# Last tile's scratch in five parts, three of them reloaded in rounds 8, 11 and 14; last inverse in 12 chunks of 512 columns, eight last output writes

## The chip, the cores and the metric

One core of a Trainium2 chip. The metric is device time of one execution in microseconds. The core's engines run side by side, each with its own queue of instructions in program order: TensorE (PE in the profile; its weight loads are PEld), VectorE (DVE), ScalarE (ACT), GpSimd (POOL) and SyncE (SP). SP issues nearly all transfers between memory and the core; ACT issues a few.

## The reference

A 7x7 circular convolution of a 224 x 224 image of 96 channels, written with FFTs:

```python
def reference(x, w):
    ...
    Xf = rfft2(x)                                # over the two image axes
    Wf = rfft2(w padded to H x W)
    Yf = jnp.einsum('bhwi,hwio->bhwo', Xf, Wf)
    y = irfft2(Yf).astype(jnp.bfloat16)
    return y
```

Inputs are `x` (1, 224, 224, 96) and `w` (7, 7, 96, 96) in bfloat16, the output has the shape of `x`.

## The kernel before

The kernel transforms along the image's height only, in 8 row blocks of 28 rows, and does the width as a short convolution with Karatsuba-like tricks. The width is cut into seven tiles (t = 0 to 6) of 32 pixels. Each tile goes through three stages:

- **a** (forward): PE multiplies pixels by the constant `Fm`; DVE and ACT cast the result from PSUM into `xf`, the spectrum. There are two `xf` buffers, used in turn.
- **b**: 17 rounds, one for each frequency pair s = 0 to 16 (`b_round`). A round is 33 small matmuls of 96 columns on PE (22 in rounds 0 and 16), a scaled copy `tt_` on ACT, the sums `u` and `v` on DVE, and a last sum into `yf` on POOL or DVE (`ydve`: on DVE in the rounds that also make the next group's differences `J`, and in the last three rounds of the last tile). Three rounds share one `yf` tile, which is written to scratch in DRAM by a transfer (`put`).
- **c** (inverse): the scratch is read back with frequency on the partitions (`tt`), PE multiplies by the constant `G`, DVE and ACT cast the result into `yo` (or free space in a `J` buffer), and SP writes the output.

Stages overlap: while tile t is in its rounds, stage a of tile t+1 and stage c of tile t-1 are run as fill jobs between the matmuls of the rounds. `add(a, b, jobs)` spreads a list of jobs over the half rounds a to b (`pace`), two half rounds to a round. `CQ` says how many leftover and how many new c jobs each tile takes; `k1` is the half round in which the last of them is due. `pump` loads `tt` tiles when buffers are free.

The last tile (t = 6, `TL`) has nobody to hide its inverse, so its stage c is special. Its scratch lies in parts of their own. Its inverse takes all 8 row blocks at once: the sum over frequencies is split into a first half (rounds 0 to 8: constant `GA`, data `tl_a`, 72 partitions, one buffer for each four row blocks g) and a second half (rounds 9 to 16: constant `GB`, data `tl_b`, 128 partitions). `tl_a` and `tl_b` lie in the `xf` buffer of tile 5, which is free by then. `GA` and `GB` are filled from `G` by small transfers, one in each round of tiles 3 and 4 (`g_parts`).

In the last tile `put` goes on ACT's queue, one round late (the list `puts`), but for the last one, which SP issues. Before, the scratch has three parts: rounds 0 to 8 (reloaded in round 11 by four transfers), rounds 9 to 14 (two transfers on ACT's queue, after the rounds) and rounds 15 and 16 (one on SP). Then come, in PE's order: eight first halves (`first`, one to each PSUM bank), `WARM` matmuls on zeros that only keep PE busy, and the loop over 16 chunks of 384 columns: `second` completes a chunk, `tail_evac` casts it on DVE or ACT in turn, the remaining first halves come as banks are freed, and every four chunks SP writes 112 partitions x 1536 columns of the output.

A transfer signals its landing on one of eight completion semaphores, which are handed out in turn to all transfers, whether SP or ACT issues them; a transfer is issued only when the previous one on its semaphore has landed.

Every instruction is recorded by one helper (line 87; 89 in the changed file), so the profile's groups are told apart by tile names.

## Time and profile before

| | |
|---|---|
| timed, median of 3 runs | 275.37 us (274.2 to 276.08) |
| span of the profiled execution | 273.5 us |
| mean granted TensorE clock | 0.998 |
| bytes moved by transfers | 46.78 MB |
| idle POOL before its sums, most of it on nothing the profile shows | 88.0 us |

The chain that ended last is 72% PE, 11% DMA, 7% DVE and 5% ACT. The stretches of the end read as follows (busy us of each engine, granted clock, bytes per time):

| stretch, us | PE | DVE | ACT | clock | GB/s |
|---|---|---|---|---|---|
| 250 to 254 | 4.00 | 3.87 | 2.41 | 1.00 | 248 |
| 254 to 256 | 0.83 | 1.07 | 0.05 | 1.00 | 301 |
| 256 to 258 | 2.00 | 0.00 | 0.00 | 1.00 | 206 |
| 258 to 260 | 2.00 | 0.00 | 0.00 | 1.00 | 90 |
| 260 to 262 | 2.00 | 0.00 | 0.00 | 1.00 | 244 |
| 262 to 264 | 0.73 | 0.00 | 0.00 | 1.00 | 69 |
| 264 to 266 | 2.00 | 1.70 | 1.34 | 1.00 | 0 |
| 266 to 268 | 2.00 | 1.69 | 1.53 | 1.00 | 227 |
| 268 to 270 | 0.20 | 0.77 | 0.77 | 1.00 | 270 |

How to read it: in a profile line the first number is the start in us from the span's start, the second the length; `out<-in` are tiles with buffer numbers left out; `xN` counts instructions; what stands in brackets is the engine's idle time before and what ended it. SPq and ACTq are the issuing queues, and their lines give the time of issuing, not of the transfer. Busy PE from 256.66 to 262.67 is the warming matmuls.

### The profile page before, as it was taken

Reading aid. Unit: us, or ns where it says so; the run is one execution under the profiler, and the core shown is the slowest. Engines: PE = TensorE matmul, PEld = TensorE weight load, DVE = VectorE, ACT = ScalarE, POOL = GpSimd, SP = SyncE. Lnnn points to the kernel's source line nnn. Section 1 sums busy time; section 2 is a strip of 40 time slices with the busy share of each in tenths; the row PEclk is TensorE's granted clock in tenths of the full one; section 3 lists DMA queues with packets and bytes.
Section 4 is the critical chain, followed back from the end, with each engine's and each line's share of the span. In section 5 each row is a group of like instructions: output and inputs, shape, how many; then the busy total and the mean of one; then the engine's idle time right before and its main releaser. Section 6 shows DMA issues by size and latency. Waiting matters only on the chain.

```text
span 273.5 us, 12147 instructions
## 1 busy us (share of the span) xinstructions
PE 259.0 (95%) x5149; PEld 237.7 (87%) x5149; DVE 213.0 (78%) x455; ACT 197.2 (72%) x485; POOL 94.8 (35%) x156
## 2 busy tenths in 40 slices
PE   8989998999999999999999999999999999899882
PEld 3659898999999989999999989999999999789661
DVE  5629799898979889779787887787977998788232
ACT  5529997668785657988988889888988865666022
POOL 7780032336446523431422222224144314224000
PEclk9999999999999999999999999999999999999999
DMA  6956110641112398996968487889678644797765
GB/s 177 222 119 169 52 47 2 168 135 48 46 47 88 105 288 149 274 263 166 310 172 248 116 228 217 200 205 313 253 194 181 204 162 132 154 297 195 196 120 180
DMA packets 46038, 46.78 MB, mean 171 GB/s; under 512 B 35150, under 2 KB 36954, under 8 KB 45886
## 3 DMA queue, kind: packets, MB, share of 16 engines
q1 hardware_dynamic: 43696, 43.94, 58.9%
q10 hardware_dynamic: 2288, 2.06, 2.7%
q8 instruction: 40, 0.66, 1.1%
q14 instruction: 14, 0.11, 0.1%
HBM read 24.65 MB, written 21.33 MB: 168 GB/s over the span
## 4 chain that ended last, share of the span: by engine, by line
PE 72%; DMA 11%; DVE 7%; ACT 5%; issue 2%; SPq 1%; POOL 1%; DVEq 0%; ACTq 0%
PE pb L87 72%; DMA wq<-in_w_dram 5%; ACT WF L87 3%; DVE WF L87 2%; DVE J L87 2%; DMA xf<-scrb 2%; DMA tt<-scr 2%; DMA scrb<-yf 1%; SPq L87 1%; DVE u L87 1%; DMA scr<-yf 1%; DVE v L87 1%; ACT xf L87 1%; DVE yf L87 1%; POOL yf L87 1%
## 5 line engine op out<-in xcount | busy, mean ns | idle before, releaser
L87 PE MATMUL pb<-WF,J 96*128 96x96 bf16 x2821 | 163.1, 206 | 1.1 <-DVE J L87 0.6
L87 PEld LDWEIGHTS <-J 96*128 96x128 bf16 x2821 | 138.2, 98 | 9.8 <-DVE u L87 1.5
L87 POOL TENSOR_TENSOR yf<-v,u 128x384 bf16<-128x384 f32 x79 | 77.8, 999 | 151.3 <-issue 88.0
L87 ACT CAST xf<-pb 96x408 bf16<-96x408 f32 (+3 forms) x143 | 67.3, 488 | 8.1 <-PE pb L87 6.3
L87 PE MATMUL pb<-WF,xf 96*128 96x96 bf16 x952 | 60.3, 206 | 1.1 <-ACT xf L87 0.5
L87 DVE TENSOR_TENSOR J<-xf 96x1824 bf16<-96x1824 bf16 (+1 forms) x84 | 57.6, 725 | 0.1
L87 PEld LDWEIGHTS <-xf 96*128 96x128 bf16 x952 | 47.3, 98 | 1.8 <-issue 0.9
L87 PE MATMUL pb<-Fm,xn 118*128 118x136 bf16 (+3 forms) x640 | 45.5, 199 | 0.9 <-DVE u L87 0.8
L87 ACT CAST WF<-pb 96x480 bf16<-96x480 f32 (+1 forms) x59 | 29.1, 573 | 6.8 <-PE pb L87 6.8
L87 PE MATMUL pb<-tt,Gm 102*84 102x384 bf16 (+1 forms) x132 | 32.4, 326 | 1.3 <-DMA tt<-scr 1.3
L87 ACT CAST J<-pb 84x384 bf16<-84x384 f32 (+1 forms) x65 | 28.0, 484 | 6.0 <-PE pb L87 3.0
L87 ACT CAST yo<-pb 84x384 bf16<-84x384 f32 (+1 forms) x66 | 28.2, 484 | 5.1 <-PE pb L87 5.1
L87 PEld LDWEIGHTS <-xn 118*128 118x128 bf16 x640 | 30.5, 97 | 1.2 <-issue 1.1
L87 DVE TENSOR_TENSOR J<-J 96x912 bf16<-96x912 bf16 (+2 forms) x42 | 22.8, 542 | 0.0
L87 PE MATMUL pb<-wq 98*128 98x120 bf16 (+1 forms) x288 | 21.3, 226 | 1.0 <-DMA wq<-in_w_dram 1.0
L87 PEld LDWEIGHTS <-wq 98*128 98x128 bf16 x288 | 19.4, 150 | 1.4 <-issue 1.4
L87 PE MATMUL pb<-wu 128*128 128x512 bf16 (+1 forms) x80 | 18.3, 392 | 1.0 <-DVE ct L87 1.0
L87 PEld LDWEIGHTS <-wu 128*128 128x128 bf16 (+1 forms) x80 | 9.4, 120 | 8.8 <-issue 3.3
L87 DVE TENSOR_TENSOR yf<-v,u 128x384 bf16<-128x384 f32 x26 | 14.7, 566 | 0.9
L87 DVE CAST WF<-pb 96x480 bf16<-96x480 f32 (+1 forms) x13 | 7.5, 610 | 6.8 <-PE pb L87 6.7
L87 PEld LDWEIGHTS <-Gm 102*84 102x84 bf16 (+1 forms) x132 | 11.0, 117 | 2.0 <-DMA tt<-scr 1.4
L87 ACT CAST tt<-pb 112x384 bf16<-112x384 f32 x8 | 3.6, 479 | 11.1 <-PE pb L87 11.0
(385 smaller groups left out, 239.7 us busy)
## 6 DMA issues: line engine op xcount, KB each, us to landing
scr<-yf SPq DMA_DIRECT2D x30, 288.0 KB
xn<-in_x_dram SPq DMA_DIRECT2D x12, 672.0 KB
tt<-scr SPq DMA_DIRECT2D x24, 336.0 KB
out_dram<-yo SPq DMA_DIRECT2D x12, 252.0 KB
out_dram<-J SPq DMA_DIRECT2D x12, 252.0 KB
tt<-scr SPq DMA_DIRECT2D x6, 288.0 KB
wq<-in_w_dram SPq DMA_DIRECT2D x1, 1719.0 KB
WF<-in_x_dram SPq DMA_DIRECT2D x2, 672.0 KB
```

Source lines behind the costliest of these rows:

```text
L87: r = fn(*a, **k)
```

## The change

The last tile's scratch is cut into five parts, rounds 0 to 5, 6 to 8, 9 to 11, 12 to 14 and 15 to 16. The first three are reloaded inside the rounds (8, 11 and 14) on SP, the fourth after the rounds on ACT's queue, the fifth on SP. The rows of `GA` and `GB` are laid out for the parts. The fill jobs of the last tile are due by half round 24 instead of 28. The last inverse works in chunks of 512 columns instead of 384, 12 instead of 16; there are 22 warming matmuls instead of 36; and each group of three chunks is written out by two transfers, one of 1024 columns and one of 512.

```diff
-SB = 15
+LPART = ((0, 6), (6, 9), (9, 12), (12, 15), (15, 17))
+LROW = (0, 48, 0, 48, 96)
+LOADS = (8, 11, 14)
...
-WARM = 36
+WARM = 22
...
             if t == TL:
-                i = (s >= SA) + (s >= SB)
-                dst, yo0 = scr_tiles[(t, i)], (0, SA, SB)[i]
+                i = next(i for i, (p0, p1) in enumerate(LPART) if p0 <= s < p1)
+                dst, yo0 = scr_tiles[(t, i)], LPART[i][0]
...
-    def load_b(i, eng, nh):
-        sb = scr_tiles[(TL, 1 + i)].rearrange("w j s (r e) -> (j s r) w e", r=2)
-        for h in range(nh):
-            w0, w1 = h * TW // nh, (h + 1) * TW // nh
-            eng.dma_start(out=tl_b[i * KB[0]:i * KB[0] + KB[i], w0:w1], in_=sb[:, w0:w1])
+    def load_l(i, eng):
+        s0, s1 = LPART[i]
+        sv = scr_tiles[(TL, i)].rearrange("w j s (r e) -> (j s r) w e", r=2)
+        halves = [(tl_a[g], g, 2) for g in range(2)] if s0 < SA else [(tl_b, 0, 1)]
+        n = NJ * 2 * (s1 - s0) // len(halves)
+        for buf, g, _ in halves:
+            eng.dma_start(out=buf[LROW[i]:LROW[i] + n].rearrange("p (w e) -> p w e", w=TW), in_=sv[g * n:(g + 1) * n])
 
     def g_parts():
-        for j in range(4):
-            dma(GA[j * 2 * SA:(j + 1) * 2 * SA, j * B:(j + 1) * B], G[0:2 * SA, 0:B])
-            yield
-        for j in range(NJ):
-            for i, (s, s1) in enumerate(((SA, SB), (SB, NS))):
-                n = 2 * (s1 - s)
-                dma(GB[i * KB[0] + j * n:i * KB[0] + (j + 1) * n, j // 4, j % 4 * B:(j % 4 + 1) * B], G[2 * s:2 * s1, 0:B])
+        for i, (s0, s1) in enumerate(LPART):
+            n = 2 * (s1 - s0)
+            for j in range(4 if s0 < SA else NJ):
+                r0 = LROW[i] + j * n
+                o = GA[r0:r0 + n, j * B:(j + 1) * B] if s0 < SA else GB[r0:r0 + n, j // 4, j % 4 * B:(j % 4 + 1) * B]
+                dma(o, G[2 * s0:2 * s1, 0:B])
                 yield
...
-        k1 = 2 * NS if t < TL else 2 * NS - 6
+        k1 = 2 * NS if t < TL else 2 * NS - 10
...
-            if t == TL and s == SA + 2:
-                sv = scr_tiles[(TL, 0)].rearrange("w j s (r e) -> (j s r) w e", r=2)
-                for g in range(2):
-                    for p0, p1 in ((0, 64), (64, KA)):
-                        dma(tl_a[g][p0:p1], sv[g * KA + p0:g * KA + p1])
+            if t == TL and s in LOADS:
+                load_l(LOADS.index(s), DE)
...
-    load_b(0, SE, 2)
-    load_b(1, DE, 1)
+    load_l(3, SE)
+    load_l(4, DE)
...
+    CW = 512
+    NC = TW2 // CW // 2
...
-        tail_evac(yo[0:M4, q % 4 * 4 * C:(q % 4 + 1) * 4 * C], pc, 4 * C)
-    order = [(g, q) for h in range(2) for g in range(2) for q in range(4 * h, 4 * h + 4)]
+        tail_evac(yo[0:M4, q % NC * CW:(q % NC + 1) * CW], pc, CW)
+    order = [(g, q) for h in range(2) for g in range(2) for q in range(NC * h, NC * h + NC)]
...
-        if q % 4 == 3:
-            w0 = TL * 2 * TW + q // 4 * PXC
-            dma(out[0, g * M4:(g + 1) * M4, w0:w0 + PXC, :].rearrange("h w c -> h (w c)"), yo[0:M4])
+        if q % NC:
+            a, b = ((0, 2 * CW), (2 * CW, 3 * CW))[q % NC - 1]
+            c0 = (TL * 2 * TW + q // NC * PXC) * C
+            dma(out[0, g * M4:(g + 1) * M4].rearrange("h w c -> h (w c)")[:, c0 + a:c0 + b], yo[0:M4, a:b])
```

More of the change, by code (lines that the diff above doesn't have):

```diff
@@ L142 @@
     KA = 4 * 2 * SA
-    KB = (NJ * 2 * (SB - SA), NJ * 2 * (NS - SB))
-    assert sum(KB) == 128
+    assert NJ * 2 * (NS - SA) == 128
     XW = 2 * TW * C
@@ L609 @@
     tl_all = xf_bufs[(TL + 1) % 2].rearrange("c p r s w j -> c (p r s w j)")
-    tl_a = [tl_all[0:KA, g * TW2:(g + 1) * TW2].rearrange("p (w e) -> p w e", e=2 * C) for g in range(2)]
-    tl_b = tl_all[:, 2 * TW2:3 * TW2].rearrange("p (w e) -> p w e", e=2 * C)
-    def load_b(i, eng, nh):
-        sb = scr_tiles[(TL, 1 + i)].rearrange("w j s (r e) -> (j s r) w e", r=2)
-        for h in range(nh):
-            w0, w1 = h * TW // nh, (h + 1) * TW // nh
-            eng.dma_start(out=tl_b[i * KB[0]:i * KB[0] + KB[i], w0:w1], in_=sb[:, w0:w1])
-    def g_parts():
-        for j in range(4):
-            dma(GA[j * 2 * SA:(j + 1) * 2 * SA, j * B:(j + 1) * B], G[0:2 * SA, 0:B])
-            yield
-        for j in range(NJ):
-            for i, (s, s1) in enumerate(((SA, SB), (SB, NS))):
-                n = 2 * (s1 - s)
-                dma(GB[i * KB[0] + j * n:i * KB[0] + (j + 1) * n, j // 4, j % 4 * B:(j % 4 + 1) * B], G[2 * s:2 * s1, 0:B])
+    tl_a = [tl_all[0:KA, g * TW2:(g + 1) * TW2] for g in range(2)]
+    tl_b = tl_all[:, 2 * TW2:3 * TW2]
+    def load_l(i, eng):
[5 more added lines that the diff above has]
+            eng.dma_start(out=buf[LROW[i]:LROW[i] + n].rearrange("p (w e) -> p w e", w=TW), in_=sv[g * n:(g + 1) * n])
+    def g_parts():
+        for i, (s0, s1) in enumerate(LPART):
[4 more added lines that the diff above has]
+                dma(o, G[2 * s0:2 * s1, 0:B])
                 yield
@@ L800 @@
             scr_tiles[t] = None
-            scr_tiles[(t, 0)] = dr_pool.tile([TW, NJ, SA, 4 * C], BF16, name="scra")
-            for i in range(2):
-                scr_tiles[(t, 1 + i)] = dr_pool.tile([TW, NJ, (SB - SA, NS - SB)[i], 4 * C], BF16, name=f"scrb{i}")
+            for i, (p0, p1) in enumerate(LPART):
+                scr_tiles[(t, i)] = dr_pool.tile([TW, NJ, p1 - p0, 4 * C], BF16, name=f"scr{'ab'[p0 >= SA]}{i}")
         else:
@@ L844 @@
     M4 = 4 * B
+    CW = 512
+    NC = TW2 // CW // 2
     def first(g, q):
-        pc = bank()[0:M4, 0:4 * C]
-        TE.matmul(pc, lhsT=GA[:], rhs=tl_a[g][:, 2 * q:2 * q + 2, :].rearrange("p w e -> p (w e)"), start=True, stop=False)
+        pc = bank()[0:M4]
+        TE.matmul(pc, lhsT=GA[:], rhs=tl_a[g][:, q * CW:(q + 1) * CW], start=True, stop=False)
         return pc
     def second(g, q, pc, yo):
-        TE.matmul(pc, lhsT=GB[:, g], rhs=tl_b[:, 2 * q:2 * q + 2, :].rearrange("p w e -> p (w e)"), start=False, stop=True)
-        tail_evac(yo[0:M4, q % 4 * 4 * C:(q % 4 + 1) * 4 * C], pc, 4 * C)
-    order = [(g, q) for h in range(2) for g in range(2) for q in range(4 * h, 4 * h + 4)]
+        TE.matmul(pc, lhsT=GB[:, g], rhs=tl_b[:, q * CW:(q + 1) * CW], start=False, stop=True)
+        tail_evac(yo[0:M4, q % NC * CW:(q % NC + 1) * CW], pc, CW)
+    order = [(g, q) for h in range(2) for g in range(2) for q in range(NC * h, NC * h + NC)]
     live = {k: first(*k) for k in order[:8]}
     for _ in range(WARM):
-        TE.matmul(live[order[7]].rearrange("p (a b) -> p a b", a=3), lhsT=wu[:, 0:M4], rhs=wu[:].unsqueeze(1).to_broadcast([128, 3, 128]),
-                  start=False, stop=False)
+        TE.matmul(live[order[7]][:, 0:384].rearrange("p (a b) -> p a b", a=3), lhsT=wu[:, 0:M4],
+                  rhs=wu[:].unsqueeze(1).to_broadcast([128, 3, 128]), start=False, stop=False)
     LF = 4
     for i, (g, q) in enumerate(order):
-        if q % 4 == 0:
+        if q % NC == 0:
             yo = t_pool.tile([128, TW // 2, 2 * C], BF16, name="tt").rearrange("p w e -> p (w e)")
```

## The prediction

> **What bounds the kernel now.** I read the page first: TensorE (PE) is busy nearly all the way, and the chain that ended last is 72% PE, so up to the last tile the kernel is PE-bound and a change to the tail can only be read in the tail.

> ```profile
> span 273.5 us, 12147 instructions
> PE 259.0 (95%) x5149; PEld 237.7 (87%) x5149; DVE 213.0 (78%) x455; ACT 197.2 (72%) x485; POOL 94.8 (35%) x156
> ```

> Then the same chain in order of time, from 200 us on (start, length, what):

> ```profile
> 226.80 2.65 DMA scr<-yf
> ...
> 229.54 4.19 DMA tt<-scr
> 233.72 0.04 issue
> 233.77 16.59 PE pb L87 x318
> ...
> 254.56 0.56 DVE yf L87
> 255.12 0.02 issue
> 255.13 4.05 DMA scrb<-yf
> 259.18 0.02 issue
> 259.20 4.70 DMA xf<-scrb
> 263.90 0.04 issue
> 263.94 3.78 PE pb L87 x21
> ```

> The tail is one line: last spectrum sum (DVE, done 255.11), its write to scratch, its reload, then the last inverse. Call the moment the inverse's second half starts T0: 263.94 here. Behind T0 the trace's completion records have the four output writes landed at 268.10, 269.87, 271.16 and 272.45, and the span ends 1.08 later. So before = T0 + 8.51 + 1.08 = 273.53. The timed median is 275.37, 1.84 above this span; I add 1.84 at the end.

> Last, the timeline of 246 to 273 us, DVE, ACT queue, PE and SP queue:

> ```profile
> 248.36 0.36 DVE L87 SCALAR_TENSOR_TENSOR u<-pb,tt__7322 128x192 f32<-128x192 f32 x1 [0.49 <-ACT tt__7322 L87]
> ...
> 252.62 0.60 DVE L87 TENSOR_TENSOR yf<-v,u 128x384 bf16<-128x384 f32 x1
> ...
> 253.31 0.33 ACTq L87 DMA_DIRECT2D scrb<-yf  x1
> ...
> 256.66 6.01 PE L87 MATMUL pb<-wu 128*112 128x384 bf16 x36
> 258.09 0.92 ACTq L87 DMA_DIRECT2D xf<-scrb  x2
> ...
> 264.30 4.47 DVE L87 CAST tt<-pb 112x384 bf16<-112x384 f32 x8 [9.19 <-PE pb L87]
> ...
> 265.39 3.76 SPq L87 DMA_DIRECT2D out_dram<-tt  x4
> ```

> To be seen: from round 12's `u` at 248.36 DVE runs almost without a hole to 255.11, so the end of the rounds is DVE's; the write of rounds 12 to 14 goes out at 253.31 and has landed when its reload starts at 258.09 (4.78); and the 36 warming matmuls cover the wait for the reload but for 1.27 us.

> **Part 1, the reload in pieces.** The final reload was 576 KB in two transfers plus 192 KB, all between 258.09 and 263.9, so the 192 KB waited behind the 576: 4.70. Now rounds 9 to 11 are fetched in round 14, and 288 + 192 KB remain. The first half of the 576 (288 KB, alone) was issued at 258.09 and had landed at 261.55, 3.46, of which its packets took some 2.1; 192 KB is two thirds, so 3.46 - 0.7 = 2.75 alone. I take 2.85, ends 2.75 and 4.70. Alone this would take 1.85 us off T0.

> **Part 2, the wait that takes its place.** Transfers of both issuing queues get eight completion semaphores in turn, and each waits until its semaphore's previous transfer has landed. The built programs' lists of waits show for the last write:

> ```
> before: SP   scrb1<-yf  128x768    waits DMAHW5, DVE
> after:  SP   scrb4<-yf  128x768    waits DMAHW1, DVE
> after:  ACT  xf<-scrb3  48x16x192  waits DMAHW5, DMAHW1
> ```

> Before, DMAHW5's previous owner was a small piece of the first reload, landed at 252.7: no wait. Before, the last write was the seventh transfer behind the write of rounds 12 to 14; in the changed program it is the eighth, so DMAHW1's previous owner is that write, from ACT's queue (its own reload waits for DMAHW1 too). So the last write may not start before that write has landed. Queued behind it on SP are its reload and all eight output writes; PE waits for them. The cover that hid the 4.78 us of that write (it ran beside the sum and the last write) is gone, and three transfers stand in a row.

> **Part 3, fourteen fill jobs two rounds earlier** (k1 28 to 24). PE's order moves them up. The first job of tile 5 stands 14 matmuls earlier, 14 x 0.042 = 0.59 us (25 matmuls start at 250.77 and the next group at 251.83), but its data lands at 233.72 as before: PE's stall there grows from 1.27 to 1.85. Two more jobs (0.33 each: one pair starts at 247.60, what follows at 247.93) now stand ahead of round 12. So round 12 starts 0.59 + 0.66 = 1.25 later; rounds 12 to 16 without fills need 168 x 0.042 = 7.1 of PE from the end of the last job, yet DVE needs its 6.75 (248.36 to 255.11) from round 12's `u` on, so DVE carries the shift through: about +1.2 for the write of rounds 12 to 14 (253.31 to 254.5) and for the last sum (256.3). Lower end +0.6, were PE's end alone to set it; no gain, since the same instructions run.

> **T0 after.** Write of 288 KB: the rows are 3.9 (issue 243.65 to the release of its reload at 247.55) and 4.78; beside it now run an output write and the 288 KB reload of round 14, much as before; 4.2. Last write, 192 KB: 2.65 (tile 5's, 226.80 in the chain, alone) to 4.05; beside it only a 288 KB reload; 2.95. Reload 2.85. T0 = 254.5 + 4.2 + 2.95 + 2.85 = 264.5, against 263.94: the wait eats the whole gain. The sum done at 256.3 has 2.4 us to spare, so Part 3's shift counts only through the first write. Ends: 253.9 + 3.9 + 2.65 + 2.75 = 263.2; 254.5 + 4.78 + 4.05 + 4.70 = 268.0.

> **Part 4, 12 chunks of 512.** DVE sets the pace before: 8 x 0.557 = 4.47 in 16 chunks. The casts of 512 elsewhere are 0.676 (DVE, x10) and 0.607 (ACT, x26): 6 x 0.676 = 4.06, 0.4 less, but it is not what ends last. The writes landed 1.29 us apart for 336 KB, so the tail behind T0 is the write stream: first issue + fixed part (268.10 - 265.39 - 1.29 = 1.42) + 4 x 1.29. The first issue comes after two casts: 0.36 + 0.05 for the longer matmul, + 0.68 and a little, 1.25 after T0 instead of 1.45. 1.25 + 1.42 + 5.16 = 7.83; the same sum gives 8.03 for before, where 8.51 was measured. I take 8.0 (7.7 to 8.8; shorter rows and four more SP issues of 0.32, which fit between casts 0.34 apart). Gain 0.5.

> [...]

> **Part 5, 22 warming matmuls for 36.** 6.01 / 36 = 0.167 each, so 3.7 in place of 6.0. The eight first halves end about 256.5 (last bank freed by the sum at 256.3), warming ends 260.15, and PE idles 4.35 us up to 264.5. What a wait costs in clock: 1.27 us cost none here. After the last matmul (ended 268.2) the stretches show

> ```profile
> 272.00:273.50 1.50, 0.00 (x0) 0.00 (x0) 0.00 (x0) 0.00 (x0) 0.00 (x0) 0.59 0.00 0
> ```

> 0.59 over 1.5 us is full clock for 0.27 and half for the rest: the clock fell at 272.27, 4.07 after. So 4.35 stands at the edge. At half clock a 512-column matmul takes 0.425 (the opening's weight loads start at 1.45, 1.88, 2.30), and it took until about 6 us, 5 us of work, to get the clock back: 5.0 + 4 x 0.215 + 0.65 for the last cast = 6.5 to the last cast instead of 4.5. The last write then issues at 6.9, + 1.42 + 0.43 for its 112 KB = 8.75 in place of 8.0.

> [...]

> **With one answer.** The small writes that fill GA and GB go from 20 to 32, the added 12 on SP in tile 4, 0.70 us each on SP there (the median of the 16 of GB), 8.4 in all: SP waits 67.8 us for POOL's sums over the kernel, which hides them; uncovered they would delay scratch writes by up to one part, 1.05. The early reloads in rounds 8, 11 and 14 block SP's queue until writes two rounds old land (1 to 3 us); behind them stand only output writes, whose buffers are not reused in those rounds.

> **The rivals.** (a) Forecast: three transfers in a row, clock kept: 264.5 + 8.0 + 1.08 = 273.6, timed 275.4. (b) Slower, the clock: once T0 is more than 4.07 after warming's end (264.2) PE starts cold: 264.5 + 8.75 + 1.08 = 274.3; with longer transfers (4.78 + 4.05 + 3.46, T0 266.8) 276.6; timed 276.2 to 278.4, middle 277. For it: the gap; against: the clock's fall has been seen once only. (c) Faster: the short rows hold, T0 263.2, gap 3.1, writes 7.8: 272.1, timed 273.9. For it: less traffic stands in the queues than before. That the wait doesn't bind at all would need the 288 KB to land in 1.8 us (254.5 to 256.3); no row is near.

> **How the numbers follow.** (a) 0.50, (b) 0.30, (c) 0.20. The before runs themselves spread 274.2 to 276.08, and 1% (2.75 us) is about what can be told from no change. Faster by over 1% (under 272.6) needs (c) and 1.3 more: 0.08. Slower by over 1% (over 278.1) needs (b) at its long end: 0.13. Within: 0.79. Range: (c) less 0.7 for the spread, 273.2, to (b)'s long end, 278.0.

> **What would show it.** SP's last scratch write issued near 258.5, 2 us after the last sum, and the wait put down to the scratch write of ACT's queue; the stall for tile 5's first tile near 1.85; T0 near 264.5; output writes landing 8 after T0; granted clock in the inverse 1.0 (a) or 0.5 (b). The prediction is wrong if the last write issues with the last sum, if T0 lies under 263, or if the last rounds take PE-bound 7 us with no shift.

## The result and the profile after

The changed kernel takes 277.96 us (median of 6 executions, 274.74 to 279.65), the kernel before 274.66 beside it (6 executions, 273.87 to 276.08). The ratio is 1.0107, interval 1.0061 to 1.0154. A second set, taken later, gave 276.78 against 274.14 with ratio 1.0097 (1.006 to 1.0133). So the change costs about 1%, some 2.7 to 2.9 us by the two ratios.

The first profile is of the longest of the six executions (279.65, which the ratio leaves out); its page and its chain of waits in order of time (start, length, what), from tile 5's first tile on:

```profile
span 277.9 us, 12119 instructions
PE 261.4 (94%) x5127; PEld 238.5 (86%) x5127; DVE 212.7 (77%) x453; ACT 197.0 (71%) x483; POOL 95.6 (34%) x156
...
PEclk9999999999999999999999999999999998699797
```

```profile
229.80 4.00 DMA tt<-scr
...
233.84 18.46 PE pb L89 x286
...
256.86 0.80 DVE yf L89
...
257.73 5.05 DMA scrb<-yf
262.78 0.02 issue
262.80 0.02 SPq L89
262.81 0.03 issue
262.84 3.22 DMA scrb<-yf
...
266.08 2.58 DMA xf<-scrb
...
268.75 3.10 PE pb L89 x13
```

Two things are to be seen. Before, one DMA write and one reload stood between the last sum and the inverse; now there are three transfers in a row, the first of them from ACT's queue, and `SPq` stands between the first and the second: SP's last write is issued 0.06 us after the write of rounds 12 to 14 has landed, 3.4 us after the last sum (done at 259.43). That is the wait of the prediction's Part 2. And the clock row has holes; in the kernel before the clock fell only at 272.29, behind the last matmul. The stretches of the same profile (from:to, length, busy time of PE, weight loads, DVE, ACT and POOL, granted clock, DMA engines busy, GB/s):

```profile
230.00:234.00 4.00, 2.18 (x43) 1.92 (x41) 3.23 (x7) 1.57 (x4) 1.51 (x2) 0.97 0.93 209
234.00:238.00 4.00, 4.00 (x38) 3.39 (x38) 1.08 (x3) 1.71 (x4) 0.99 (x1) 0.50 0.61 159
238.00:242.00 4.00, 4.00 (x53) 3.58 (x52) 1.29 (x4) 1.75 (x5) 0.99 (x1) 0.67 0.92 223
...
262.00:264.00 2.00, 2.00 (x8) 1.31 (x7) 0.00 (x0) 0.00 (x0) 0.00 (x0) 0.50 0.10 7
```

In 234 to 238 TensorE is busy for all 4 us but does 38 matmuls at clock 0.50; 82 fit in the same stretch of the kernel before, 78 and 75 in that of two further profiles below. The clock fell at 233.78, at the end of the stall for tile 5's first tile, and that makes this execution's last sum 3 us late. It fell again at 261.09, just ahead of the warming matmuls, which start at 261.12.

The second profile is of the second set's shortest execution, 275.22, and kept its clock up to 261.31, past the landing of the last scratch write; it is the one to set beside before. Its chain:

```profile
252.91 2.46 DMA scrb<-yf
...
255.39 0.02 SPq L89
...
255.43 3.94 DMA scrb<-yf
...
259.40 2.61 DMA xf<-scrb
...
262.10 6.20 PE pb L89 x14
```

The same three transfers, here quicker, but the inverse behind them takes 6.20 us in place of 3.10. Its stretches say why:

```profile
260.00:262.00 2.00, 0.00 (x0) 0.00 (x0) 0.00 (x0) 0.00 (x0) 0.00 (x0) 0.83 0.37 98
262.00:264.00 2.00, 1.91 (x5) 1.10 (x6) 1.06 (x2) 0.59 (x1) 0.00 (x0) 0.50 0.00 0
264.00:266.00 2.00, 2.00 (x7) 0.95 (x6) 1.02 (x2) 1.17 (x2) 0.00 (x0) 0.50 0.56 172
266.00:268.00 2.00, 2.00 (x6) 1.03 (x5) 0.79 (x2) 0.59 (x1) 0.00 (x0) 0.50 0.58 173
```

TensorE's last warming matmul ended at 258.65, it idled 3.45 us, the clock fell at 261.31 and came back at 268.13, so nearly the whole second half of the inverse ran at half clock. At tile 5's stall (1.55 us here) the clock stayed at 1.00.

Executions differ long before the change: in the ten profiles of the table below tile 5's stall ends between 231.88 and 235.33, and in the two with four parts and late fills, whose programs are the same up to there, at 232.21 and 235.33, so the absolute times of two profiles can't be set side by side. All comparisons below count from the end of that stall, where TensorE's first matmul on that tile starts. The start of the stall will not do: with early fills it lies 14 matmuls, 0.59 us, earlier in the order of TensorE's work. T0 is, as in the prediction, the start of the inverse's second half; "inverse" is T0 to the landing of the last output write, "end" from there to the end of the span. "Late" and "early" say when the fill jobs are due; before has them late, the changed kernel early.

```
kernel (warming matmuls)      stall  last sum  T0 after  inverse  end   total from
                                     at        the sum                  the stall's end
before (36)                   1.27   21.34     8.83      8.51     1.08  39.76
predicted                     1.85   22.5      8.2       8.0      1.08  39.8
changed, second profile (22)  1.55   22.56     7.49      9.97     1.44  41.46
changed, first profile (22)   1.82   25.59     9.33      7.74     1.44  44.10
changed, 44 warming           1.90   22.63     8.26      7.67     1.44  39.99
before, fills early (36)      2.02   22.52     6.97      8.50     1.09  39.08
before, new inverse (36)      1.03   21.34     7.45      7.64     0.90  37.33
four parts (22)               1.41   22.39     8.10      9.01     1.08  40.57
four parts (32)               1.43   22.87     7.03      7.85     1.08  38.83
four parts, fills late (22)   1.06   21.33     8.97      9.98     1.26  41.54
four parts, fills late (30)   1.00   21.33     6.76      7.84     1.25  37.18
```

Between before and the changed kernel's second profile the 1.70 us are: last sum +1.22, T0 behind the sum -1.34, inverse +1.46, end +0.36. These are two executions, and T0 behind the sum scatters from one to the next (see "The base" below): the table shows where the time went in them, not what each part is worth in the median. What lengthens the end is not shown.

### The profile page after: what moved, and what is told of

Read it like the earlier page. It is cut to its first block, busy times and chain, and to the rows that moved or that the text cites. A ratio compares the mean times of both kernels' runs of the same rounds, so it can differ in the third digit from the quotient of the medians.

```text
span 277.9 us, 12119 instructions
## 1 busy us (share of the span) xinstructions
PE 261.4 (94%) x5127; PEld 238.5 (86%) x5127; DVE 212.7 (77%) x453; ACT 197.0 (71%) x483; POOL 95.6 (34%) x156
## 3 DMA queue, kind: packets, MB, share of 16 engines
HBM read 24.65 MB, written 21.33 MB: 165 GB/s over the span
## 4 chain that ended last, share of the span: by engine, by line
PE 71%; DMA 11%; DVE 7%; ACT 4%; issue 2%; SPq 1%; POOL 1%; DVEq 0%; ACTq 0%
PE pb L89 71%; DMA wq<-in_w_dram 5%; DMA scrb<-yf 3%; ACT WF L89 3%; DVE J L89 2%; DVE WF L89 2%; DMA tt<-scr 1%; DVE v L89 1%; DVE u L89 1%; SPq L89 1%; DMA scr<-yf 1%; DMA xf<-scrb 1%; ACT xf L89 1%; DVE yf L89 1%; POOL yf L89 1%
## 5 line engine op out<-in xcount | busy, mean ns | idle before, releaser
L89 PE MATMUL pb<-WF,J 96*128 96x96 bf16 x2821 | 164.9, 207 | 1.1 <-DVE J L89 0.6
L89 PEld LDWEIGHTS <-J 96*128 96x128 bf16 x2821 | 140.0, 98 | 10.4 <-issue 1.6
L89 PEld LDWEIGHTS <-xf 96*128 96x128 bf16 x952 | 47.9, 99 | 1.8 <-issue 0.9
L89 PE MATMUL pb<-tt,Gm 102*84 102x384 bf16 (+1 forms) x132 | 33.5, 335 | 1.8 <-DMA tt<-scr 1.8
L89 PE MATMUL pb<-wu 128*128 128x512 bf16 (+1 forms) x66 | 17.2, 429 | 1.1 <-DVE ct L89 1.1
L89 PEld LDWEIGHTS <-wu 128*128 128x128 bf16 (+1 forms) x66 | 8.5, 131 | 8.8 <-issue 2.7
L89 DVE CAST tt<-pb 112x512 bf16<-112x512 f32 x6 | 3.8, 686 | 9.9 <-PE pb L89 9.9
```

The lines of the kernel that those rows point to most:

```text
L89: r = fn(*a, **k)
```

## The experiments

Three theories were on the table after the first profile. A: the early fills starve TensorE at tile 5's stall, its clock falls there, and everything behind it is late. B: the last scratch write, tied to the landing of the write of rounds 12 to 14, costs the time. C, rival (b) of the prediction: the inverse starts at half clock because 22 warming matmuls leave TensorE idle too long. Granted clocks of whole executions are means over the span; a mean of 0.995 or more leaves at most some 3 us at half clock in a span of 273 us (before's profile: 0.998, full clock up to 272.29), and is called a kept clock below.

**Fills late (e1).** The changed kernel with the last tile's fill jobs spread as before.

```
-        k1 = 2 * NS if t < TL else 2 * NS - 10
+        k1 = 2 * NS if t < TL else 2 * NS - 6
```

> The changed kernel with the last tile's fill jobs due by half round 28 again, nothing else undone. Theory A (clock: the earlier fills lengthen PE's stall at tile 5's first tile from 1.27 to 1.82 us, the clock falls to half there for 6.8 us, and this is most of what the change lost): stall back to about 1.3, clock 1.0 through all rounds, last sum done near 255.3 instead of 259.4, timed 274 to 275.5, within 1% of before. Theory B (the last scratch write standing behind the landing of the one before is what costs): the last sum may move, but the time stays near 277 to 278, since the last write is still behind that landing (now through an output write ahead of it on SP).

Measured: 279.42 (4 executions), ratio 1.0189 (1.0093 to 1.0286): slower still. The stall was 1.13 us, the clock stayed at 1.0 there, the last sum came at 254.93, and yet T0 was 12.0 us behind that sum. The chain of this kernel:

```profile
253.12 4.22 DMA scrb<-yf
...
257.41 0.34 SPq L89
...
257.80 0.37 SPq L89
...
258.26 5.64 DMA scrb<-yf
...
263.91 2.94 DMA xf<-scrb
...
266.94 5.59 PE pb L89 x13
```

Three issues of SP follow the landing at 257.34 (the two `SPq` pieces and the write behind them): with late fills an ordinary output write has become the eighth transfer behind the write of rounds 12 to 14 and inherits its semaphore. The output write waits, and the round-14 reload and the last write queue behind it; all then run at once, and the last write takes 5.64. So this run does not settle A: the stall is cured, but T0 has moved further behind the sum. The price of the wait was not the same in the two kernels, T0 12.0 us behind the sum here and 7.49 and 9.33 in the changed kernel, which differ in which transfer draws the shared semaphore and what stands behind it.

**Fills early in the kernel before (e4).** The opposite edit of the same line in the kernel before (6 to 10), nothing else.

> The kernel before with one line of the change: the last tile's fill jobs due by half round 24. Theory A: stall near 1.85 us at tile 5's first tile, clock at half for about 6.8 us behind it in most executions, last sum done near 259, T0 near 268, timed 277 to 279. Theory B: only the shift of the fills themselves, 0.6 to 1.2 us: 275 to 276.5.

Measured: 275.04 (10 executions) against 274.62, ratio 1.0044 (1.0 to 1.0087). The stall was 2.02 us, the longest of all profiles, at full clock. From the stall's end the last sum came 1.18 later than before, and the last write then took 1.85 us in place of 4.05:

```profile
256.19 1.85 DMA scrb<-yf
...
258.06 4.94 DMA xf<-scrb
```

So early fills delay the sum by what was predicted (1.18 for 1.2). Whether the short write belongs to them is not shown: with before's fills and the new inverse it took 2.71.

**Warming in the stall (e9).** The changed kernel, with ten warming matmuls put into the first inverse job of tile 5, ahead of its first matmul, to keep TensorE busy in the stall.

```
-                        pb = bank()[0:nj * B, 0:4 * C]
+                        pbk = bank()
+                        if (t, gi, h, q, b) == (TL - 1, 0, 0, 0, 0):
+                            for _ in range(10):
+                                TE.matmul(pbk[0:M4W, 0:384].rearrange("p (a b) -> p a b", a=3), lhsT=wu[:, 0:M4W],
+                                          rhs=wu[:].unsqueeze(1).to_broadcast([128, 3, 128]), start=True, stop=True)
+                        pb = pbk[0:nj * B, 0:4 * C]
```

> The changed kernel with ten warming matmuls (1.6 us) put on PE just ahead of the first inverse matmul of tile 5, so that PE is busy while it waits for the same data at the same time. Theory A: the data still arrives near 233.8 and PE goes on then, but the clock stays 1.0; last sum done near 256.4, timed 274.5 to 276. If the wait itself and not the clock is what costs, nothing changes: last sum near 259.4, timed 277.5 to 278.5.

Measured: 277.14 (4 executions), ratio 1.0127 (1.0051 to 1.0203): no gain. The clock held at the stall, so A falls as the main cause; and the inverse was cold (it ran at half clock) all the same: a gap of 3.41 us ahead of T0, clock 0.5 from 266.43 to 269.85. In this profile the clock also fell at 20.67, in the weight transforms, as it did in profiles of two kernels that have before's fills (with the inverse alone, and with four parts and late fills): those falls belong to no edit.

**The last write on ACT's queue (e2).** The changed kernel with the last scratch write issued by ACT, and the reload of rounds 9 to 11 moved from SP in round 14 to ACT behind the rounds.

```
-                put()
+                put(SE if t == TL else DE)
...
-            if t == TL and s in LOADS:
+            if t == TL and s in LOADS[:2]:
...
+    load_l(2, SE)
     load_l(3, SE)
```

> The changed kernel with the last scratch write issued by ACT, where it finds a free completion semaphore, and the reload of rounds 9 to 11 moved behind it on ACT's queue; early fills kept. Theory B: the last write issues within 0.3 us of the last sum instead of 3.4 us after it; T0 lies 7 us after the last sum instead of 9.3; timed about 2 us under the changed kernel, 275.5 to 276.5. Theory A alone: the clock still falls at tile 5's stall, last sum still near 259; if the wait costs nothing the time stays near 278.

Measured: 275.68 (10 executions), ratio 1.0066 (1.0015 to 1.0118), against 1.0097 to 1.0107 for the changed kernel. The last write is issued 0.03 us after the last sum and lands in 1.96 us; but the reloads, now side by side, stretch the last one to 5.43:

```profile
255.79 1.96 DMA scrb<-yf
...
257.82 5.43 DMA xf<-scrb
```

T0 is 7.57 us behind the sum, the gap 2.94 by the profile's idle time (the expectation below of 36 warming matmuls has 3.02), and the inverse cold. B's wait is real and was removed, but T0 came no sooner behind the sum than in the changed kernel's second profile (7.49): the crowded reload took what the wait had cost.

**The changed kernel again (e10) and with 44 warming matmuls (e11).** The first unchanged, the second with `WARM = 44`.

> The changed kernel once more, unchanged, for a second profile. Theory B (the last scratch write cannot be issued before the write of rounds 12 to 14 has landed): put 4 is issued within 0.2 us after that landing, at least 1.5 us after the last sum, as in the first profile (3.4 us). Theory C (the inverse starts at half clock, because TensorE idles between the last warming matmul and the last reload): the idle gap ahead of the inverse's second half is 3 to 4.5 us, the granted clock is 0.5 for at least 2 us behind it, and the last output write lands 9.0 us or more after the start of the inverse's second half. Theory A (the clock falls at tile 5's stall): the clock stands at 0.5 somewhere between 231 and 241 us; if it does not and the time is still 276.5 to 278, A falls for good. Time by all three 277 to 278.

> The changed kernel with 44 warming matmuls in place of 22: 22 x 0.167 us = 3.7 us less idle time ahead of the inverse, nothing else moved. Theory C: the clock stays at 1.0 through the inverse, the last output write lands about 8.0 us after the start of its second half, and the time is 1.2 to 2.0 us under the changed kernel (275.9 to 276.8 if that stands at 278). Theory B alone (the time is lost in the chain of writes ahead of the inverse, and the clock behind it does not matter): same as the changed kernel within 0.5 us.

The first gave the second profile above. A is not needed there: the clock was kept at the stall and the set's median is 276.78 all the same, though in longer executions of the set a fall at the stall is not excluded. B holds, with a wait of 0.8 us behind the sum where 1.5 was the expected least, and C holds: gap 3.45, inverse 9.97. With 44, in a profile with T0 8.26 behind the sum:

```profile
262.00:264.00 2.00, 1.32 (x8) 0.81 (x7) 0.00 (x0) 0.00 (x0) 0.00 (x0) 1.00 0.34 91
264.00:266.00 2.00, 2.00 (x11) 1.13 (x10) 1.93 (x4) 1.62 (x3) 0.00 (x0) 1.00 0.14 37
```

Full clock, 11 matmuls in 2 us where the cold inverse did 7, the inverse 7.67. Timed 276.03, ratio 1.0062 (1.002 to 1.0104): 0.75 us less in the medians where 1.2 to 2.0 were expected, and the two intervals overlap. The mechanism is seen in the trace; its worth in the timed median is not resolved.

**ACT's queue with 36 warming matmuls (e12).**

> The kernel of e2 (last scratch write and third reload issued by ScalarE) with 36 warming matmuls in place of 22, which takes 14 x 0.167 = 2.3 us of the 3.02 us gap that stood ahead of the inverse in its profile. Theory C: the clock stays at 1.0 through the inverse, the last output write lands about 8 us after the start of the second half in place of 9.10, and the time is 1.0 to 1.5 us under e2: 274.2 to 274.7 against 274.6 before. B alone: as e2, 275.7.

Missed: 276.39, ratio 1.005 (1.0006 to 1.0094), no better than with 22. The profile, of an execution of 278.65, over 2 us longer than the median, shows what long warming risks:

```profile
257.00:260.00 3.00, 1.93 (x5) 1.12 (x6) 0.00 (x0) 0.00 (x0) 0.00 (x0) 0.50 0.97 218
260.00:264.00 4.00, 4.00 (x14) 2.62 (x14) 0.00 (x0) 0.00 (x0) 0.00 (x0) 0.53 0.78 149
264.00:268.00 4.00, 4.00 (x26) 3.17 (x25) 0.00 (x0) 0.00 (x0) 0.00 (x0) 1.00 0.00 0
```

The reload of rounds 6 to 8 could start only at 254.71, 0.02 us after the scratch write of rounds 9 to 11, whose semaphore it had drawn, landed; five of the eight first halves waited for it, TensorE idled 2.63 us ahead of them, and the clock fell at 256.94. The warming then ran at half speed and held TensorE until 267.81, with the last reload landed at 264.15: 3.66 us lost to the remedy.

**The inverse alone (e6).** The kernel before with only the 12 chunks of 512 and the eight writes.

```
+    CW = 512
+    NC = TW2 // CW // 2
...
+        if q % NC:
+            a, b = ((0, 2 * CW), (2 * CW, 3 * CW))[q % NC - 1]
```

> The kernel before with only the inverse of the change (12 chunks of 512 columns, eight output writes), its scratch in three parts, its fills and its 36 warming matmuls as before. By the prediction's Part 4: the last landing comes 8.0 us after the start of the inverse's second half in place of 8.51, so 0.5 us under the kernel before (274.1 against 274.6). A rival: four more writes of the output on SP's queue and shorter rows cost as much as the chunks save, and the time is the same within 0.2 us.

Measured: 273.56 (12 executions) against 274.14, ratio 1.0012 (0.9978 to 1.0047). In the trace the inverse is 7.65 us in place of 8.51, a little better than predicted. The timed medians move the same way by 0.58, but the ratio of 1.0012 does not, and it cannot be told from 1.

**Four parts in place of five (e13, e16, e14, e15).** Rounds 0 to 8 are one part, reloaded by two transfers in round 11 in place of four in rounds 8 and 11. In the order as built three or four transfers then stand between the write of rounds 12 to 14 and the last one, in place of seven (two reloads are gone, and output writes have moved ahead of the first), so the two no longer share a semaphore, and no queue is changed.

```
-LPART = ((0, 6), (6, 9), (9, 12), (12, 15), (15, 17))
-LROW = (0, 48, 0, 48, 96)
-LOADS = (8, 11, 14)
+LPART = ((0, 9), (9, 12), (12, 15), (15, 17))
+LROW = (0, 0, 48, 96)
+LOADS = (11, 14)
...
-    load_l(3, SE)
-    load_l(4, DE)
+    load_l(2, SE)
+    load_l(3, DE)
```

With 22 warming matmuls, with 32, with the fills late as well, and with fills late and 30:

> The changed kernel with its scratch in four parts in place of five: rounds 0 to 8 are one part, reloaded in two transfers in round 11, so two transfers fewer stand between the write of rounds 12 to 14 and the last scratch write, and that one no longer shares a completion semaphore with it. Theory B: the last scratch write is issued within 0.1 us of the last sum (0.8, 2.4 and 3.4 us in three profiles of the changed kernel and its warm form), T0 comes at the last sum + 6.5 to 7.5, and the time is 1 to 2.5 us under the changed kernel. Theory C: of this the idle gap ahead of T0 still decides a part: under 2 us of gap the inverse runs at full clock, over 3 us at half. A rival: without the wait the last write and its reload share the DMA engines with the write of rounds 12 to 14 and its reload, both take longer (4 to 5 us in place of 2 to 3), and the time is the changed kernel's within 0.5 us.

> As the kernel in four parts, with 32 warming matmuls in place of 22 (10 x 0.167 = 1.7 us less gap). Theory C: the inverse runs at full clock in most executions, the last landing comes 7.7 us after T0, the time is 0.5 to 1.5 us under the four-part kernel with 22. If the four-part kernel's gap is already under 2 us: the same, or slower where the warming outlasts the last reload.

> The four-part kernel with the fill jobs of the last tile spread to 28 as before (22 warming matmuls). Early fills cost 0.4% in the kernel before; here: last sum about 1 us earlier, but TensorE's fills end no earlier, so 0.5 to 1.2 us under the four-part kernel. A rival as in the first such experiment: an output write that still waits for TensorE's late fills stands ahead of the last scratch write on SP's queue, and the gain is lost.

> Four parts, fills as before, 30 warming matmuls: the version meant to beat both. Last sum at 255.1 in the time of the kernel before, T0 at 261.5 to 262.5, last landing 7.7 us later, span 270.6 to 271.6 against 273.5, so 272.0 to 273.5 us timed beside 274.1 to 274.6 of the kernel before. If the last write and reload are stretched by the other transfers, T0 is at 263.5 and the time that of the kernel before.

```
kernel                          median   beside before  ratio   interval
changed (e10)                   276.78   274.14         1.0097  1.0060 to 1.0133
four parts, 22 (e13)            275.88   273.44         1.0061  1.0024 to 1.0097
four parts, 32 (e16)            274.94   273.44         1.0045  1.0013 to 1.0077
four parts, fills late, 22 (e14) 273.56  273.44         0.9987  0.9954 to 1.0020
four parts, fills late, 30 (e15) 273.14  273.44         0.9991  0.9964 to 1.0019
```

The chain of the four-part kernel with late fills and 22 warming matmuls, in the longest of its twelve executions (275.46):

```profile
252.99 0.56 DVE yf L89
...
253.57 5.08 DMA scrb<-yf
...
258.66 3.75 DMA xf<-scrb
...
262.51 6.04 PE pb L89 x14
```

The write of rounds 12 to 14 is gone from the chain: the last write follows the last sum by 0.02 us. With early fills it comes 1.16 and 0.41 us behind the sum, because SP's queue is still held by the round-14 reload, which waits for the data of the write of rounds 9 to 11; the expected 0.1 was missed there. The inverse is cold again behind a gap of 3.69 us. Thirty warming matmuls end that:

```profile
262.94 0.48 issue
263.42 3.31 PE pb L89 x14
```

The gap is 0.48, the inverse 7.84, and the profile's total from the stall's end is 37.18, the least of all; but the kernel before with the new inverse alone has 37.33, so the cut scratch shows no gain of its own.

What follows from the four: with the sharing gone, moving the fills back is worth 0.0074 of the time, 2.0 us where 0.5 to 1.2 were expected, and the two intervals do not touch. The last sum accounts for 1.06 us of it (22.39 to 21.33 in the table); where the rest comes from is not shown. Breaking the sharing alone (1.0097 to 1.0061) and more warming (1.0061 to 1.0045, 0.9987 to 0.9991) are each within their intervals. The last version was meant to beat both kernels. It beats the changed one; against the kernel before it is the same within what can be measured.

## Why the prediction was partly right

The range (273.2 to 278.0) held the time, and "within 1%" was given 0.79 for a change that landed on the edge of it: 277.96 lies 0.04 under the upper end, which is luck; the second set's 276.78 lies well inside. But the likeliest case, (a) at 275.4 with the clock kept, is not what happened: the time is that of rival (b), whose middle was 277.

**Part 1, the last reload: right.** 2.85 was taken; 2.58, 2.61 and 2.65 were measured in the changed kernel and its form with 44.

**Part 2, the wait: right in kind and in its sum.** The last write was issued 0.06 us behind the landing of the write from ACT's queue in all three of those profiles, 0.8, 2.4 and 3.4 us behind the last sum where 2.2 was predicted. Its three transfers scatter (5.05, 4.05 and 2.46 for the first; 3.22, 3.08 and 3.94 for the second; predicted 4.2 and 2.95), T0 behind the sum is 7.5 to 9.3, predicted 8.2. T0 itself came at 268.75, 262.10 and 263.64 where 264.5 was forecast, and "under 263" had been named as a sign of being wrong; in the execution with 262.10 the stall had ended 1.72 us sooner than in before's, so counted from the same moment T0 is at 263.8. Why the program has such a wait is not shown: no run here took the wait away from a shared semaphore; the four-part runs only changed which transfers share.

**Part 3, early fills: right.** The stall was put at 1.85 and is 1.55 to 1.90. The last sum was to come 1.2 later behind the landing of tile 5's first tile; in the eight profiles with early fills and full clock at the stall it came 1.05 to 1.53 later behind the stall's end, 1.22 in the mean, while all five with late fills have 21.33 or 21.34. The timed price with the sharing gone is 2.0 us. And "Part 3's shift counts only through the first write" left out that late fills have a price of their own in the five-part kernel (the first experiment): fills and sharing cannot be priced apart. The 12 added small writes of tile 4 show no delay: with early fills the stall began at 230.50 to 232.06 in five profiles with the five parts, and at 231.62 in before with early fills.

**Part 4, the inverse: right.** First issue 1.26 after T0 (predicted 1.25), DVE's cast of 512 at 0.686 (predicted 0.676), inverse 7.67 and 7.74 at full clock (predicted 8.0).

```profile
L89 DVE CAST tt<-pb 112x512 bf16<-112x512 f32 x6 | 3.8, 686 | 9.9 <-PE pb L89 9.9
```

**Part 5, the warming: the step that failed.** The prediction set the fall of the clock at 4.07 us after the last matmul, from the one fall in the trace, called the 4.35 us gap "at the edge", and gave the cold inverse 0.30 and a price of 0.75 us. Of seven profiles with 22 warming matmuls six have a cold inverse, behind gaps of 2.68, 2.94, 3.41, 3.45, 3.69 and 6.24 us; the seventh, the first profile above, had a gap of 2.23. None of the seven profiles with 30 or more has one. Cold, the inverse takes 8.91 to 9.98; with the same 12 chunks and the clock kept, 7.59 to 7.85. So the price is 1.1 to 2.4 us. Three terms made the predicted price too small. From the issue of the last write to its landing the prediction took 1.42 + 0.43 = 1.85, and 2.32 to 2.62 were measured behind a cold start. That issue, put at 6.9 after T0, came at 6.47 to 6.52 in the three profiles whose clock was half for 3.41 us, but at 7.42 to 7.64 in the three with 6.83. And the inverse at full clock, from which the price is counted, was put at 8.0. The single fall seen, 4.07 us after the last matmul, was a poor reason to call 4.35 the edge: the gaps of 2.68 and 2.94 us were cold too.

**A clock fall at tile 5's stall: not foreseen.** A stall of 1.82 us was enough for it in one profile; 1.90, 1.93 and 2.02 us in others were not. In that one the last sum came 25.59 us behind the stall's end in place of 22.56, some 3 us later.

**The base.** The sum was made against from a profile of before whose last write took 4.05 us and whose T0 lay 8.83 behind the sum. Two other kernels with before's scratch had 1.85 and 2.71 for that write, T0 6.97 and 7.45 behind the sum. Of 89 executions of before beside the experiments, 51 kept the clock (mean 0.995 or more), with a median of 273.32, some 2 us under the 275.37 that I added to. A forecast equal to that profile was therefore already a forecast of a loss against the typical execution, which the prediction did not see.

The clock is also where most of the timed difference shows. By mean granted clock, the executions (with the median time of each class in us) are:

```
                     0.995 up      0.990-0.995  0.985-0.990  0.980-0.985  under 0.980
before, 89           51 (273.32)   19 (274.33)  12 (275.61)  7 (277.11)   -
changed, 18          -             1 (274.74)   4 (276.63)   9 (277.25)   4 (279.56)
changed, 44 warm, 12 4 (274.44)    3 (275.81)   3 (276.85)   -            2 (280.12)
four, late, 30, 12   6 (272.24)    3 (273.17)   2 (275.54)   1 (274.22)   -
```

Not one execution of the changed kernel kept its clock. At equal clock it stands 0.1 to 1.0 us over before in the three classes that both have. This is a sorting by something that the kernel itself influences, so it is evidence for the clock's part (A's fall at the stall and C's cold inverse together) and no measurement of it. With the clock kept, the version with four parts, late fills and 30 warming matmuls is 1.1 us under before.

What stays open: how much of the 2.7 us is the clock and how much the fills. The single steps overlap within their intervals but for the fills, and the parts depend on each other.

## What to carry to other kernels

Before splitting a transfer, list which transfers inherit which completion semaphore: here one transfer more between two writes (the eighth in place of the seventh) tied the last one to another queue (issued 0.06 us after the write there had landed), and three or four fewer freed it (with late fills, 0.02 us behind the sum). Fill a wait of TensorE up to the moment the data lands, with a margin for short DMAs only: here too few warming matmuls cost 1.1 to 2.4 us behind the wait, too many at half clock cost 3.66. Price a tail from more than one execution, since the same last write took between 1.85 and 4.05 us in kernels with the same scratch.
